# A fused attention and expert kernel: a new written-out order of its work

## The chip, the cores and the metric

The kernel runs on one core of a Trainium2 chip. The core has five engines with a queue each: PE (matrix products, results to PSUM), DVE and ACT (both read PSUM and the on-chip memory), POOL (here: loads and masks) and SP (here: stores). Each takes its instructions in the order of its own list and waits at semaphores for what another engine or a transfer has to finish first. The metric is the device time of the whole program in microseconds: a median of 178.3 over three runs of the kernel before (176.12 to 179.82).

## The reference

Two stages, for a batch of 8 with 576 positions. The first is an attention with 8 heads of 64, whose keys and values are means over groups of 8 positions (576 become 72):

```python
k_p = k.reshape(B, H, Sp, pool, D).mean(axis=3)
v_p = v.reshape(B, H, Sp, pool, D).mean(axis=3)
scores = scale * np.matmul(q, k_p.transpose(0, 1, 3, 2))
...
return np.matmul(attn, v_p)
```

Its output x (8 x 576 x 512) goes through four causal attention experts, of which each position uses the two with the largest gate:

```python
logits = x @ w_gate
topk = np.argpartition(-logits, K, axis=-1)[..., :K]
...
for e in range(E):
    q, k, v = x @ wq[e], x @ wk[e], x @ wv[e]
    scores = np.where(causal, -1e9, scale * (q @ k.transpose(0, 2, 1)))
    ...
    ye = a @ v @ wo[e]
    out += (gate weight of e, or 0) * ye
```

## The kernel before, in words

The batches are worked one after the other, but overlapping: while the experts of one batch run, the first attention of the next two or three is under way. All operations stand as tokens in one string, SEQ, and a loop over it issues them; the order in SEQ is the order in every engine's list, and no scheduler changes it. The semaphores between engines are put in from the data that the operations share. A token is a name, its arguments, the batch behind the colon, a PSUM bank (or a pair) behind the @, and a letter d where DVE is to do what otherwise ACT does. The names, with their lines:

- L_k, L_q, L_v (L118): loads of raw K, V (three each a batch) and q (four), cast to bf16 on the way, issued by POOL. Three raw buffers of each kind go round. In the kernel before the four loads of q of batch 0 are cut in halves, L_q00 to L_q31. W (L131) are the loads of the weights. The loads take eight semaphores in turn, so that each waits for the load eight before it to have landed.
- PK, PV: products on PE that form the means of K and V; kc and vc bring them out of PSUM. KT, kt: K turned on PE, and its copy. u (L251): q turned on DVE, one half of the heads each.
- E0, E1, E2: scores of the first attention (two groups of heads, then the tail of both); e (L277, L270): their exponentials on ACT. D, d, x: sums of the exponentials on PE, then ln and exp(-ln) on ACT (L298, L302). O, o: product with V, and scaling into x transposed on DVE (L321, L314).
- c0 to c4 (L177): weights put into the order that the products read, in the kernel before on ACT.
- P, p: projections to q and k of the experts. V, v: values and gate. g: the gate's small operations on DVE.
- S, s (L437, L431): scores of the experts for pair ep and column group ti (as in S02), and their exponentials on ACT; a (L454, L446): the causal masks on the diagonal blocks, on POOL. B with bz, bg, b: product with V on PE (for a pair and a part of the rows), normalisation and gate on DVE. A product B needs the masks of the diagonal blocks that its rows touch.
- T, t: turning for the last product. Y, y: the last product and its copy to a store buffer, from which SP (at the very end ACT too) stores.
- H (L174): n products of a zero tile of 512 columns, without a use for their result.
- I, J, K, M: constants and padding.

POOL's list thus holds loads and masks in one row: a mask that stands behind a load isn't done before that load is issued. The loop that reads a token ends so:

```python
            elif name == "H":
                warm_up(*a, int(bank))
            ...
            elif name in MATRIX:
                where = tuple(int(x) for x in bank) if name == "E" else int(bank)
                at[b, name, a] = where
                cut[0] = bool(tiled)
                MATRIX[name](b, where, *a)
```

## Time and profile before

| | us |
|---|---|
| median of three runs | 178.3 (176.12 to 179.82) |
| profiled execution | 177.88 |
| its span | 176.2 |
| PE busy in it | 153.7 |
| ACT busy | 140.4 |
| DVE busy | 125.4 |
| POOL busy | 92.8 |

The span runs from the first to the last instruction on the core; the time of an execution is a little longer. Matrix products are pipelined, so a busy PE need not be PE at its peak: the clock that it was granted stands in a row of its own, in tenths of full speed. "Idle before" names who released an engine that waited. A row of a timeline gives start, length, engine, line, operation, output and input, and how many instructions are merged; a row of groups gives busy time and the mean of one instruction in ns. In the list of transfers the last number is the time from issue to landing.

### The profile page before, as it was taken

The numbers are of one execution on the slowest core, as the hardware profiler recorded it, in microseconds if no ns is written. First come the engines' busy times: TensorE is split into PE (matmuls) and PEld (weight loads), VectorE is DVE, ScalarE is ACT, GpSimd is POOL, SyncE is SP. The second block draws the span as 40 slices with busy tenths as digits, with TensorE's granted clock in tenths as the row PEclk, the third lists the DMA queues.
The fourth block names the chain that finished last, engine by engine and source line by source line (L and its number), as shares of the span: only waits on it lengthen the run. The fifth ranks groups of instructions, "written<-read, shape, count | busy, mean of one in ns | idle before, by whom it ended". The sixth has DMA issues, their size and how long they took to land.

```text
span 176.2 us, 5231 instructions
## 1 busy us (share of the span) xinstructions
PE 153.7 (87%) x2028; PEld 83.9 (48%) x2028; DVE 125.4 (71%) x404; ACT 140.4 (80%) x257; POOL 92.8 (53%) x166
## 2 busy tenths in 40 slices
PE   7288798998950899999999999999999999989960
PEld 2023343454520474754455656664457556546630
DVE  1330433594860579898999999999888769999960
ACT  2025989999970388999999999989899999989760
POOL 7889577677597988977468402401303054422000
PEclk9957999999998589999999999999999999999999
DMA  3999999999999998999999921002011020169894
GB/s 31 166 104 155 179 180 180 179 185 181 180 181 180 173 119 85 142 193 211 209 181 209 182 66 61 4 0 65 0 63 60 30 93 6 70 242 347 274 339 168
DMA packets 65577, 24.99 MB, mean 142 GB/s; under 512 B 60688, under 2 KB 60944, under 8 KB 65552
## 3 DMA queue, kind: packets, MB, share of 16 engines
q0 software_dynamic: 60304, 15.21, 88.2%
q1 hardware_dynamic: 5024, 9.05, 14.6%
q10 hardware_dynamic: 224, 0.39, 0.7%
q8 instruction: 16, 0.26, 0.6%
q14 instruction: 9, 0.07, 0.1%
HBM read 30.42 MB, written 9.44 MB: 226 GB/s over the span
## 4 chain that ended last, share of the span: by engine, by line
PE 60%; ACT 12%; DVE 10%; DMA 7%; issue 4%; POOL 2%; ACTq 0%; DVEq 0%; POOLq 0%
PE psum L186 54%; DMA vraw<-in_v_dram 4%; DMA kraw<-in_k_dram 4%; PE psum L195 3%; ACT etb L437 3%; ACT eta L277 3%; PE psum L174 3%; DVE ofin L177 2%; ACT rza L302 2%; ACT rza L298 2%; DVE qk L177 1%; POOL kraw L118 1%; DVE osc L493 1%; DVE gt L488 1%; POOL vraw L118 1%
## 5 line engine op out<-in xcount | busy, mean ns | idle before, releaser
L437 ACT ACTIVATE etb<-psum 128x1024 bf16<-128x1024 f32 x48 | 46.8, 1032 | 1.8 <-PE psum L186 1.4
L454 POOL TENSOR_SCALAR_AFFINE_SELECT etb<-etb 128x256 bf16<-128x256 bf16 x64 | 25.0, 409 | 39.6 <-ACT etb L437 39.0
L277 ACT ACTIVATE eta<-psum 96x1024 bf16<-96x1024 f32 x32 | 31.1, 1022 | 2.5 <-PE psum L186 2.3
L186 PE MATMUL psum<-vaug,etb 128*128 128x65 bf16 x480 | 21.1, 195 | 7.2 <-POOL etb L454 6.6
L118 POOL DMA_DIRECT2D qraw<-in_q_dram x36 | 23.3, 655 | 5.2 <-DMA vraw<-in_v_dram 1.6
L186 PEld LDWEIGHTS <-etb 128*128 128x128 bf16 x480 | 18.7, 99 | 14.1 <-POOL etb L454 7.3
L186 PE MATMUL psum<-wvg,xT 128*128 128x260 bf16 x144 | 22.0, 285 | 0.6 <-ACT wvg L177 0.5
L118 POOL DMA_DIRECT2D kraw<-in_k_dram x24 | 18.6, 781 | 7.2 <-PE psum L186 2.3
L118 POOL DMA_DIRECT2D vraw<-in_v_dram x24 | 18.5, 772 | 6.7 <-PE psum L186 2.1
L177 DVE CAST qk<-psum 128x512 bf16<-128x512 f32 (+1 forms) x26 | 17.0, 653 | 7.0 <-PE psum L186 5.9
L321 DVE TENSOR_TENSOR xT<-psum,rza 128x512 bf16<-128x512 f32 x32 | 20.6, 682 | 1.5 <-ACT rza L302 1.3
L186 PE MATMUL psum<-wop,oT 128*128 128x512 bf16 (+1 forms) x74 | 20.1, 373 | 0.2 <-DVE qk L177 0.2
L186 PE MATMUL psum<-xT,wkp 128*128 128x512 bf16 (+1 forms) x128 | 19.4, 286 | 0.3 <-ACT eta L277 0.3
L186 PE MATMUL psum<-xT,wqp 128*128 128x512 bf16 (+1 forms) x128 | 19.5, 286 | 0.1
L493 DVE TENSOR_TENSOR osc<-psum,gt 128x256 bf16<-128x256 f32 (+2 forms) x40 | 16.9, 424 | 1.4
L186 PEld LDWEIGHTS <-xT 128*128 128x128 bf16 x144 | 13.0, 100 | 8.2 <-issue 4.9
L186 PE MATMUL psum<-qk 64*128 64x64 bf16 (+4 forms) x192 | 16.1, 284 | 0.4 <-DVE kp L177 0.3
L177 ACT COPY ofin<-psum 128x512 f32<-128x512 f32 (+1 forms) x24 | 13.9, 590 | 3.1 <-PE psum L186 2.1
L251 DVE STREAM_TRANSPOSE qT<-qraw 128x576 f32<-128x576 f32 x16 | 12.0, 765 | 5.4 <-DMA qraw<-in_q_dram 5.4
L186 PE MATMUL psum<-qT,kpT 32*96 32x512 bf16 (+1 forms) x256 | 13.7, 312 | 0.6 <-ACT etb L437 0.6
L486 DVE RECIPROCAL rzb<-psum 128x4 f32<-128x4 f32 (+2 forms) x40 | 6.8, 173 | 9.3 <-PE psum L186 8.4
L174 PE MATMUL psum<-warm 128*128 128x512 bf16 x34 | 12.0, 498 | 1.6 <-DVE onesd L147 1.3
(78 smaller groups left out, 240.2 us busy)
## 6 DMA issues: line engine op xcount, KB each, us to landing
out_dram<-ofin SPq DMA_DIRECT2D x31, 256.0 KB, 3.4
kraw<-in_k_dram POOLq DMA_DIRECT2D x24, 192.0 KB, 7.6
vraw<-in_v_dram POOLq DMA_DIRECT2D x24, 192.0 KB, 7.3
qraw<-in_q_dram POOLq DMA_DIRECT2D x28, 144.0 KB, 7.9
out_dram<-ofin SPq DMA_DIRECT2D x7, 128.0 KB, 2.8
qraw<-in_q_dram POOLq DMA_DIRECT2D x8, 72.0 KB, 4.7
wst_q<-in_moe_wq_dram POOLq DMA_DIRECT2D x1, 256.0 KB, 6.6
wst_k<-in_moe_wk_dram POOLq DMA_DIRECT2D x1, 256.0 KB, 7.4
```

Source lines behind the costliest of these rows:

```text
L118: nc.gpsimd.dma_start(out=dst, in_=src)
L174: nc.tensor.matmul(out=psum[:, bank, :], lhsT=warm[:, 0:128], rhs=warm[:], start=True, stop=True)
L177: (nc.vector.tensor_copy if dve else nc.scalar.copy)(out=out, in_=in_)
L186: nc.tensor.matmul(out=out, lhsT=lhsT, rhs=rhs, start=start, stop=stop)
L195: nc.tensor.transpose(out=out[s], in_=in_[:, s], identity=ident[0:n, 0:n])
L251: nc.vector.transpose(out=dst.rearrange("p (a s n) -> p a n s", s=32, n=2), in_=src.rearrange("p (a n d) -> p a n d", n=2, d=32))
L277: nc.scalar.activation(out=eta[:, h : h + 3 : 2, 0:MAIN], in_=psum[0:KR, bank : bank + 2, :], func=EXP, scale=ATT_EXP_SCALE,)
L321: nc.vector.tensor_tensor(out=xT[:, 2 * g + t, mcols(b)], in0=psum[:, bank, :], in1=rz[:, g, 0:MAIN], op=MULT)
L437: nc.scalar.activation(out=et[:, ep, :, eo : eo + n], in_=psum[:, bank : bank + 2, 0:n], func=EXP, scale=MOE_EXP_SCALE,)
L454: nc.gpsimd.affine_select(out=blk, in_=blk, pattern=[[0, 2], [1, 128]], compare_op=ISGE, fill=0.0, base=0, channel_multiplier=-1,)
L486: nc.vector.reciprocal(out=rz, in_=o[:, :, :, HD : HD + 1])
L493: nc.vector.tensor_tensor(out=oscs[ep][:, own, :].rearrange("p c (e d) -> p e c d", e=2), in0=o[:, :, :, 0:HD], in1=gt.to_broadcast([128, ...
```

## The change

SEQ is replaced by another order of nearly the same tokens. What differs in kind:

- q of batch 0 comes in four loads, as for the other batches, not in eight halves.
- The weights' loads W1 to W4 stand elsewhere: W1 behind K of batch 1, W2 to W4 ahead of K of batch 2.
- c0 to c4 carry the d: DVE does them.
- Eighteen H products stand first on PE, then 3 and 10 around the turning of K; 39 in all instead of 34. A new mark c on an H token makes the product small: only the last 32 rows of the bank are written.
- Masks stand singly between loads: from batch 0 on, a row of loads is broken by the masks that are ready there.
- B10 of batch 0 stands ahead of PV of batch 2 and PK of batch 3; before, B00 was the first product B, behind PK of batch 3.
- The rest is placed anew all the way through, with other PSUM banks and other shares of ACT and DVE in the copies. The last tokens, from the last row of blocks on, are nearly the same.

```diff
--- before.py
+++ after.py
@@ -169,9 +169,10 @@
             nc.vector.memset(etbs[1 - h][64 * h : 64 * h + 64, :, :, 1536:1600], 0.0)
 
 
-    def warm_up(n, bank):
+    def warm_up(n, bank, low):
+        rows = slice(KR, 128) if low else slice(0, 128)
         for _ in range(n):
-            nc.tensor.matmul(out=psum[:, bank, :], lhsT=warm[:, 0:128], rhs=warm[:], start=True, stop=True)
+            nc.tensor.matmul(out=psum[rows, bank, :], lhsT=warm[:, rows], rhs=warm[:], start=True, stop=True)
 
     def copy(dve, out, in_):
         (nc.vector.tensor_copy if dve else nc.scalar.copy)(out=out, in_=in_)
@@ -553,73 +554,72 @@
              "d": (dn, "D"), "o": (ov, "O"), "v": (vg, "V"), "p": (p, "P"), "s": (sb, "S"),
              "t": (t, "T"), "y": (y, "Y")}
...
-        I:0 L_k0:0 L_k1:0 L_k2:0 J:0 K:0 M:0 L_q00:0 L_q10:0 H8:0@0 L_q20:0 L_q30:0 L_q01:0 L_q11:0 L_q21:0 PK:0@0
-        L_q31:0 H3:0@1 L_v0:0 kc:0 KT:0@0 L_v1:0 u0:0 H2:0@1 kt:0 L_v2:0 E0:0@02 W0:0 H7:0@4 e01:0 W1:0 u1:0 e00:0
-        L_k0:1 E1:0@24 E2:0@06 L_k1:1 e21:0 e10:0 L_k2:1 e20:0 L_q0:1 D0:0@2 e11:0 PV:0@3 L_q1:1 D2:0@0 d0:0 D1:0@1
-        vc:0d L_q2:1 H1:0@4 x0:0 c0:0 O01:0@3 L_q3:1 d1:0 O00:0@2 O20:0@4 o01:0 O10:0@5 x1:0 O11:0@6 L_v0:1 H8:0@1
-        o00:0 d2:0 x2:0 L_v1:1 o11:0 o10:0 L_v2:1 c1:0 P_q0:0@5 L_k0:2 c2:0 o20:0 c3:0 L_k1:2 P_k0:0@4 p_q0:0 L_k2:2
-        P_t0:0@6 p_k0:0 PK:1@5 L_q0:2 p_t0:0 S00:0@0 L_q1:2 kc:1 S03:0@2 S01:0@6 s03:0 KT:1@5 L_q2:2 s00:0 S02:0@2
-        kt:1d H5:0@4 L_q3:2 s01:0 u0:1 W2:0 s02:0 u1:1 E0:1@04 W3:0 e01:1 E1:1@26 W4:0 e11:1 L_v0:2 P_k1:0@4 L_v1:2
-        e10:1 D1:1@5 p_k1:0d PV:1@6 L_v2:2 d1:1 P_q1:0@7 vc:1d e00:1 L_k0:3 E2:1@24 O10:1@6 p_q1:0d L_k1:3 x1:1 O11:1@0
-        D0:1@1 e21:1 o11:1 L_k2:3 PK:2@7 e20:1 d0:1 D2:1@2 O01:1@3 o10:1 L_q0:3 O00:1@0 d2:1 O20:1@1 x2:1 S12:0@4 kc:2d
-        x0:1 L_q1:3 o20:1 s12:0 S11:0@6 o01:1 L_q2:3 P_t0:1@1 o00:1 s11:0 S10:0@2 L_q3:3 KT:2@4 u0:2 P_k1:1@0 p_t0:1
-        L_v0:3 kt:2 u1:2 s10:0 P_k0:1@1 L_v1:3 c4:0 p_k1:1 L_v2:3 E1:2@46 p_k0:1d V3:0@2 L_k0:4 e11:2 V2:0@0 v3:0d
-        L_k1:4 V2:1@1 e10:2 v2:0d E0:2@26 v2:1d L_k2:4 V1:0@0 e01:2 L_q0:4 V0:0@1 v1:0d P_q0:1@4 e00:2 L_q1:4 v0:0d
-        g1:0 E2:2@06 L_q2:4 g2:0 g0:0 D1:2@5 p_q0:1 g3:0 PV:2@2 g4:0 g5:0 e21:2 L_q3:4 g6:0 D0:2@4 e20:2 g7:0 V0:1@3
-        vc:2d d0:2 L_v0:4 V1:1@0 d1:2 v0:1d V3:1@4 L_v1:4 g8:0 x1:2 g9:0 S03:1@2 v1:1d S02:1@6 O10:2@5 x0:2 a02:0 v3:1d
-        O00:2@0 O01:2@1 s03:1 o10:2 a00:0 PK:3@4 s02:1 a01:0 O11:2@2 o01:2 D2:2@5 a12:0 P_q1:1@3 kc:3 o00:2 L_v2:4 d2:2
-        o11:2 B00:0@1 V4:1@0 p_q1:1 a11:0 bz00:0 S00:1@4 bg00:0 a10:0 b00:0 v4:1 S12:1@2 S10:1@6 u0:3 a03:0 s00:1
-        V3:2@1 L_k0:5 g1:1 B01:0@0 g2:1 v3:2 L_k1:5 KT:3@4 g3:1 s10:1 V0:2@5 g4:1 bz01:0 bg01:0 P_q0:2@1 b01:0 a02:1
-        v0:2d s12:1 kt:3d a10:1 B12:0@0 p_q0:2d L_k2:5 V1:2@4 g0:1 x2:2 S11:1@2 bz12:0 g5:1 v1:2 a12:1 S01:1@6 g6:1
-        g7:1 T01:0@1 s11:1 g8:1 B10:0@5 g9:1 P_k1:2@4 a00:1 bg12:0 t01:0d b12:0 a03:1 bz10:0 s01:1 bg10:0 a11:1 b10:0
-        E0:3@02 L_q0:5 p_k1:2d B02:0@5 e01:3 u1:3 T12:0@6 a01:1 P_k0:2@7 L_q1:5 bz02:0 e00:3 bg02:0 B11:0@4 b02:0
...
-        Y3:7@7 ya4:7 yb4:7d Y2:7@6 y3:7 y2:7dp z2:7
+        I:0 H18:0@0 L_k0:0 L_k1:0 L_k2:0 J:0 K:0 M:0 L_q0:0 L_q1:0 L_q2:0 L_q3:0 L_v0:0 L_v1:0 L_v2:0 PK:0@0 W0:0
+        H3:0@1 kc:0 L_k0:1 KT:0@0 H10:0@1 L_k1:1 kt:0 L_k2:1 u0:0 W1:0 u1:0 E0:0@02 L_q0:1 E1:0@46 e00:0 H3:0@0c L_q1:1
+        e11:0 PV:0@0 L_q2:1 e10:0 H2:0@0c vc:0d e01:0 D0:0@1 c0:0d O01:0@0 L_q3:1 O00:0@4 c1:0d d0:0 D1:0@5 E2:0@26
+        x0:0 L_v0:1 O11:0@1 d1:0 o01:0 e21:0 L_v1:1 O10:0@5 x1:0 o00:0 e20:0 o10:0 O20:0@4 L_v2:1 D2:0@0 PK:1@2 o11:0
+        d2:0 kc:1 P_q0:0@5 x2:0 c2:0d W2:0 o20:0 P_k0:0@2 c3:0d p_q0:0 W3:0 P_t0:0@4 p_k0:0 W4:0 KT:1@5 p_t0:0 kt:1d
+        S00:0@0 L_k0:2 S02:0@2 P_k1:0@5 s00:0 u1:1 L_k1:2 s02:0 u0:1 a00:0 E1:1@06 L_k2:2 p_k1:0d H2:0@4 e10:1 a02:0
+        E0:1@24 e11:1 L_q0:2 H1:0@2c PV:1@0 L_q1:2 e00:1 P_q1:0@1 vc:1d e01:1 E2:1@26 L_q2:2 c4:0d D0:1@0 e20:1 O01:1@4
+        L_q3:2 p_q1:0d d0:1 D1:1@5 V2:0@2 e21:1 L_v0:2 d1:1 V1:0@3 v2:0d x0:1 V0:0@6 L_v1:2 v1:0d x1:1 S10:0@0 o01:1
+        D2:1@2 O11:1@3 v0:0 O00:1@5 d2:1 L_v2:2 V3:0@7 o11:1 x2:1 s10:0 O20:1@2 o00:1 O10:1@6 PK:2@3 L_k0:3 o20:1 v3:0
+        S03:0@4 S11:0@0 kc:2d P_t0:1@2 s03:0 L_k1:3 s11:0 o10:1 V4:1@7 L_k2:3 KT:2@3 p_t0:1d S01:0@4 v4:1 kt:2d S12:0@0
+        g1:0 L_q0:3 P_k1:1@2 s01:0 g2:0 u0:2 L_q1:3 s12:0 P_k0:1@3 u1:2 a10:0 E0:2@46 p_k1:1 L_q2:3 p_k0:1d g0:0 V1:1@0
+        a11:0 e00:2 g3:0 P_q0:1@1 g4:0 L_q3:3 v1:1d e01:2 g5:0 a12:0 E1:2@24 g6:0 g7:0 g8:0 L_v0:3 B10:0@0 g9:0 p_q0:1d
+        e10:2 V3:1@6 bz10:0 PV:2@7 L_v1:3 bg10:0 b10:0 e11:2 D0:2@1 vc:2d a03:0 V2:1@2 L_v2:3 d0:2 v3:1d T10:0@0 V0:1@3
+        v2:1d a01:0 x0:2 E2:2@46 t10:0d O10:2@1 L_k0:4 v0:1d e21:2 D1:2@0 O01:2@2 e20:2 g1:1 O11:2@3 d1:2 L_k1:4
+        O00:2@6 o01:2 D2:2@7 PK:3@4 x1:2 o00:2 L_k2:4 P_q1:1@0 d2:2 kc:3 o10:2 L_q0:4 x2:2 B01:0@2 o11:2 p_q1:1 S00:1@4
+        L_q1:4 g0:1 S02:1@6 u0:3 S11:1@0 s00:1 P_q0:2@3 u1:3 L_q2:4 s02:1 V0:2@4 bz01:0 bg01:0 a00:1 P_k1:2@5 b01:0
+        s11:1 L_q3:4 v0:2d p_q0:2d T01:0@2 a02:1 KT:3@4 p_k1:2 S03:1@6 S12:1@0 kt:3d B12:0@3 s03:1 L_v0:4 t01:0d g2:1
+        s12:1 S10:1@4 bz12:0 S01:1@6 g3:1 L_v1:4 PV:3@2 g4:1 g5:1 s10:1 g6:1 O20:2@0 P_k0:2@1 a03:1 vc:3d L_v2:4 s01:1
+        o20:2 B11:0@2 g7:1 a12:1 g8:1 B02:0@0 p_k0:2 g9:1 bz11:0 E0:3@46 bg11:0 L_k0:5 b11:0 B00:0@1 bg12:0 bz02:0
+        e00:3 P_q1:2@2 b12:0 L_k1:5 bz00:0 bg02:0 bg00:0 b02:0 b00:0 PK:4@3 e01:3 L_k2:5 p_q1:2d E1:3@04 L_q0:5 kc:4d
+        V2:2@2 e10:3 L_q1:5 u0:4 P_t0:2@3 a11:1 T00:0@6 v2:2d B01:1@7 p_t0:2 L_q2:5 t00:0d e11:3 T12:0@0 T11:0@1
+        T02:0@2 D0:3@3 t12:0d t11:0d a10:1 Y1:0@6 t02:0d bz01:1 d0:3 L_q3:5 bg01:1 KT:4@2 b01:1 V3:2@4 y1:0 kt:4d a01:1
...
+        T11:7@7 t12:6d t01:7d y0:7 Y4:7@0 t11:7d Y3:7@3 ya4:7 yb4:7d Y2:7@2 y3:7 y2:7dp z2:7
...
@@ -639,7 +639,7 @@
             elif name == "z":
                 z(b, *a, nc.scalar)
             elif name == "H":
-                warm_up(*a, int(bank))
+                warm_up(*a, int(bank), bool(tiled))
             elif name in "IJK":
                 setup_consts("IJK".index(name))
             elif name == "M":
```

## The prediction

> **What bounds the kernel now.** First the page: its shares, then its forty slices of 4.4 us.

> ```profile
> span 176.2 us, 5231 instructions
> ...
> PE 153.7 (87%) x2028; PEld 83.9 (48%) x2028; DVE 125.4 (71%) x404; ACT 140.4 (80%) x257; POOL 92.8 (53%) x166
> ...
> PE   7288798998950899999999999999999999989960
> ...
> PEclk9957999999998589999999999999999999999999
> DMA  3999999999999998999999921002011020169894
> ```

> The shares name PE, but the slices tell more: from the fifteenth slice on PE is full, and what is lost is lost ahead of it (slices 1 to 4, a zero in slice 13) and in the last two. The granted clock is low in slices 3 and 4 and again in 13 and 14, each time after PE stood still. The DMA engines are full up to slice 22. So I cut the span into stages at events of the trace: K of batch 0 landed (9.33), the first projection (23.66), the pooling of K of batch 3 (49.23), the end of the hole (57.66), the last matmul (170.42). The columns are length, busy time of PE, of PE's weight loads, DVE, ACT and POOL, then clock, DMA share and GB/s.

> ```profile
> 0.00:9.33 9.33, 4.35 (x11) 1.32 (x12) 2.45 (x17) 1.28 (x1) 7.08 (x15) 0.95 1.05 102
> 9.33:23.66 14.33, 12.39 (x116) 4.67 (x115) 4.88 (x8) 9.56 (x17) 11.77 (x16) 0.79 1.54 149
> 23.66:49.23 25.57, 23.76 (x293) 11.94 (x295) 15.41 (x45) 24.46 (x44) 17.57 (x25) 1.00 1.80 181
> 49.23:57.66 8.43, 1.85 (x27) 0.80 (x20) 2.35 (x4) 2.51 (x6) 7.04 (x13) 0.91 1.82 180
> 57.66:63.00 5.34, 5.27 (x43) 3.22 (x44) 3.06 (x13) 2.77 (x7) 5.12 (x11) 0.50 1.54 150
> 63.00:70.00 7.00, 6.80 (x84) 3.81 (x82) 6.42 (x24) 5.58 (x11) 6.11 (x12) 1.00 1.07 104
> 70.00:110.00 40.00, 39.98 (x624) 22.69 (x623) 37.52 (x115) 38.62 (x72) 23.32 (x41) 1.00 1.31 162
> 110.00:153.00 43.00, 42.73 (x638) 25.42 (x637) 37.26 (x118) 40.31 (x73) 11.58 (x29) 1.00 0.11 35
> 153.00:170.42 17.42, 16.54 (x209) 9.98 (x207) 15.38 (x66) 14.72 (x32) 3.18 (x8) 1.00 0.84 296
> 170.42:176.20 5.78, 0.00 (x1) 0.00 (x0) 0.69 (x1) 0.58 (x1) 0.00 (x0) 0.95 0.57 194
> ```

> Each stage has its own limit. Up to 23.66 a chain over all engines begins with the first loads. From 23.66 to 49.23 it is ACT (24.46 of 25.57 busy) with the DMA queue close behind at a steady 181 GB/s. Then comes a hole: 8.43 us in which PE works 1.85, so 6.58 idle. After it PE runs 5.34 us at half its clock, and from 63 on PE is the limit, idle only 0.20 + 0.02 + 0.27 + 0.88 = 1.4 us until the last matmul. The timelines of PE and POOL, one row of ACT's and one piece of the chain of waits say what the hole is.

> ```profile
> 50.04 1.04 PE L186 MATMUL psum<-xT,wqp 128*128 128x512 bf16 x4
> 57.66 0.76 PE L186 MATMUL psum<-vaug,etb 128*128 128x65 bf16 x6 [6.58 <-POOL etb L454]
> ...
> 39.31 1.06 ACT L437 ACTIVATE etb<-psum 128x1024 bf16<-128x1024 f32 x1
> ...
> 47.27 6.77 DMA vraw<-in_v_dram
> ...
> 54.61 0.77 POOL L118 DMA_DIRECT2D vraw<-in_v_dram  x1 [0.70 <-DMA vraw<-in_v_dram]
> 55.68 0.77 POOL L118 DMA_DIRECT2D vraw<-in_v_dram  x1 [0.30 <-issue]
> 56.45 2.22 POOL L454 TENSOR_SCALAR_AFFINE_SELECT etb<-etb 128x256 bf16<-128x256 bf16 x6
> ```

> PE stands before B00:0, the first product of the second attention, which needs the causal masks of batch 0. ACT had the last exponentials of that batch ready at 40.4. The masks are POOL's, and POOL works in order: ahead of them stood loads, each waiting until the load eight before it has landed. At 54.61 it still waits for a V load; only at 56.45 come six masks in 2.22 us. So the masks came some 16 us after their data.

> **The change part by part.** My sum goes along the stages, against the profiled execution's 177.88 us (span 176.2 and 1.68 around it); the median of the runs shown, 178.3, is 0.4 us above it.

> *The start.* These rows, of PE, DVE and ACT, carry it.

> ```profile
> 1.26 3.60 PE L174 MATMUL psum<-warm 128*128 128x512 bf16 x8 [1.26 <-DVE onesd L147]
> 9.33 1.01 PE L186 MATMUL psum<-kraw,poolk 96*32 96x512 bf16 x4 [2.41 <-DMA kraw<-in_k_dram]
> 21.67 1.89 PE L174 MATMUL psum<-warm 128*128 128x512 bf16 x8 [0.34 <-ACT rza L298]
> ...
> 12.52 0.78 DVE L251 STREAM_TRANSPOSE qT<-qraw 128x576 f32<-128x576 f32 x1 [0.87 <-DMA qraw<-in_q_dram]
> ...
> 13.98 1.93 ACT L277 ACTIVATE eta<-psum 96x1024 bf16<-96x1024 f32 x2 [1.41 <-PE psum L186]
> 19.34 0.61 ACT L298 ACTIVATE rza<-psum 128x512 f32<-128x512 f32 x1
> ```

> Eighteen warm-ups stand first in place of eight. Eight took 3.60 us cold and eight 1.89 us at full clock; some eight at 0.45 and ten at 0.24 end near 7.3, before K has landed at 9.33, so they block nothing. They take away the long idle time after which slices 3 and 4 ran slow. With K at 9.33 the four left pooling matmuls (0.5 at full clock instead of 1.01), kc and the flips end near 10.8; then ten warm-ups by 0.24 hold PE until 13.2. The q loads are four instead of eight: the same bytes and half the issues, but the first turn now waits for both halves. At 9.33 us 0.95 MB had moved (102 GB/s); K and q of a batch are 1.18 MB, so at 149 to 181 GB/s they are through near 10.8, landed near 12, and two turns by 0.78 end at 13.5. So E0 starts at 12.8 to 13.2, is over near 13.9, and the exponentials begin where they do now (13.98): nothing gained, and 1 us lost if q lands a microsecond later.

> Behind that the order changes. Now six exponentials stand ahead of d0 at 19.34, with waits for cold PE work between them; in the new order four stand there, by 0.95 some 3.9 us: d0 at 18.0, 1.3 us earlier. The weight casts c0 to c4 leave ACT for DVE:

> ```profile
> L177 ACT COPY wqp<-wst_q 128x512 bf16<-128x512 bf16 x2 | 1.2, 602 | 0.0
> L177 ACT COPY wkp<-wst_k 128x512 bf16<-128x512 bf16 x2 | 1.1, 613 | 0.0
> L177 ACT COPY wvg<-wst_v 128x1024 bf16<-128x1024 bf16 x1 | 1.1, 1074 | 0.0
> L177 ACT COPY wvg<-wst_g 128x16 bf16<-128x16 bf16 x1 | 0.2, 243 | 0.0
> ```

> One of them, 0.6, stands between x0 and d1 in the chain. P_q0:0 thus starts some 2.0 us earlier, at 21.7; ends 0 (q late) and 3. DVE has room for the casts: 4.88 us busy in 14.33 and 15.41 in 25.57. DVE's price for them isn't in the trace; between nothing and ACT's it changes nothing under that cover.

> *From the first projection to the pooling of K of batch 3.* ACT is the limit, and it loses c2, c3 and the two casts of c4 here: 1.2 + 1.1 + 0.2 = 2.5 us. The rest of its list is much the same: two evictions of q or k, a kc and a kt go, three V evictions come. The queue allows that gain and no more:

> ```profile
> kraw<-in_k_dram POOLq DMA_DIRECT2D x24, 192.0 KB, 7.6
> vraw<-in_v_dram POOLq DMA_DIRECT2D x24, 192.0 KB, 7.3
> qraw<-in_q_dram POOLq DMA_DIRECT2D x28, 144.0 KB, 7.9
> wst_q<-in_moe_wq_dram POOLq DMA_DIRECT2D x1, 256.0 KB, 6.6
> ```

> A batch is 3 x 192 + 4 x 144 + 3 x 192 = 1728 KB, the weights 1028; up to K of batch 3 that is 3 x 1728 + 1028 + 576 = 6788 KB or 6.95 MB. From 0.95 MB at 9.33, at 181 GB/s, it is there at 42.5; if the dip to 149 GB/s before 23.66 recurs, 2.5 us later. ACT would come there at 49.23 - 2.0 - 2.5 = 44.7, between the two. I take -2.5; ends 0 and -3.5.

> *The hole.* Between the loads the list of POOL now has masks. B10:0 comes first, ahead of V of batch 2, and needs the masks a10 and a11 of batch 0; these stand behind two loads of q of batch 3 and a third, which wait for the last of q and the first of v of batch 2. Bytes to there: 2 x 1728 + 1152 + 192 + 1028 = 5828 KB, 5.97 MB: 9.33 + 5.02 / 0.181 = 37.1, or 39.6 with the dip, and about 1 us for issue and mask. PE gets there with 5.6 us of ACT's work still to do before K of batch 3, at 39 to 40. The wait is thus between 0 and 2 us, not 6.58. B00:0 comes only some 13 us later. No load behind them waits longer on that account: a mask is 2.22 / 6 = 0.37 us and the queue has eight loads in it. I take the 6.58 off, and the slow clock with it: 5.27 us at 0.50 hold 2.6 us of work. Together -9.2; ends 0, where the same hole is somewhere else, and -9.2.

> [...]

> *What is late next.* From K of batch 3 to the last matmul PE works 1.85 + 5.27 + 6.80 + 39.98 + 42.73 + 16.54 = 113.2 us, 110.6 at full clock; the tokens behind that point are nearly the same ones (31 projections in both, 49 score groups for 47, 27 V for 28, 39 products B for 40). That it could be fed with 1.4 us of idle time was helped by the hole, in which loads ran on. Without it ACT has about 105 us to do in those 112, DVE little less, and three engines so close will wait for one another. I add 2 us; ends 0 and 7. The loads don't limit it: 1.77 MB a batch take 9.8 us, PE needs some 17. SP's stores are the same forty, behind the same evictions, and the last 5.78 us, stores included, are the same tokens.

> Sum: 177.9 - 2.0 - 2.5 - 9.2 + 2.0 = **166.2**. From the other side: 44.7 + 110.6 + 1.4 + 2.0 + 5.8 + 1.7 = 166.2.

> **The rivals.**

> *Half the gain.* The loads set the pace up to batch 3 and PE waits for them and for the masks behind them: the queue dips as it does now (149 GB/s), K of batch 3 is there at 45 to 47, B10:0 waits 2 us, and the later masks, again placed between waiting loads (batch 1's behind q and v of batch 4), cost 2 to 3 more. For it: POOL is still in order and every load still waits for one. Against: the bytes are as early as PE. 166.2 + 5 = 171.

> *No change.* The hole only moves: PE is as late at its next bound, ACT and the loads. 178. Against it: 6.58 us in which ACT was idle too (2.51 busy of 8.43), and loads twice as fast as PE.

> *Slower.* One mechanism: the masks of B10:0. Now PE first needs a mask at 51.1 (50.04 + 1.04), in the new order at 39 to 40. If the loads ahead of the masks land x us late, PE stands there for x and the slow clock (2.6) is back; and the queue being late by as much, it comes again at the masks of batch 1, likewise between loads: 166.2 + 2 (x + 2.6). It decides from x = 5 (181.4, 2% above); at the 6.58 of now it gives 184.6. Nothing in the rows shows such a delay at a steady 181 GB/s.

> *The change doesn't do what it says*: the lists of instructions show the masks between the loads, so that falls under the second.

> **How the numbers follow.** 0.62 for the forecast (162 to 169), 0.23 for half the gain (169 to 174), 0.08 for no change, 0.07 for slower. The predicted time is 166; from 161.5 to 174 are the first two, with 0.16 left out and a little below. The low end is all ends at their best: 177.9 - 3 - 3.5 - 9.2 = 162.2. Two per cent, about what a measurement of this kernel can tell from no change, is 3.6 us: faster 0.86, same 0.07, slower 0.07.

> **What would show it.** PE without an idle time over 3 us between 13 and 150 us, the granted clock at 1.00 from 6 us on; P_q0:0 near 21.7, K of batch 3 pooled near 44.7, B10:0 near 40 with under 2 us of wait for POOL; last matmul near 158. I am wrong if a wait of PE for masks or K/V loads over 3 us stands between 25 and 60, if ACT waits long for PE before 45, or if PE is idle by more than 6 us in all behind 45.

## The result and the profile after

The kernel after takes 163.32 us (median of four runs, 163.03 to 163.7) against 177.75 for the kernel before beside it (176.12 to 179.82): a ratio of 0.922, with a 95% interval of 0.914 to 0.929. That is 13.9 us less by the ratio, where 12 had been forecast. The profiled execution took 163.38 us. Here and below, ratios leave out a run over 1.5% longer than the quickest of its kernel, while medians and ranges keep it.

The page of the kernel after: span, shares, and the forty slices, now 4.04 us each.

```profile
span 161.7 us, 5222 instructions
...
PE 150.5 (93%) x2033; PEld 83.1 (51%) x2033; DVE 124.1 (77%) x411; ACT 136.3 (84%) x250; POOL 90.4 (56%) x162
...
PE   6896699899999999999999999999999999999950
...
PEclk9999858999999999999999999999999999999996
DMA  2999999999999999999999920101141122357894
```

The zero of slice 13 is gone, and PE is full from the ninth slice on. Two things differ from what was expected: PE is not quite full before that, and the clock is low again, in slices 5 to 7. I cut the span at the same events as before, this time K of batch 0 at 8.32, the first projection at 20.95, the pooling of K of batch 3 at 46.78 and the last matmul at 155.75. The columns are length, busy PE, weight loads, DVE, ACT, POOL, then clock, DMA share and GB/s.

```profile
0.00:8.32 8.32, 6.30 (x21) 2.27 (x21) 2.45 (x17) 1.28 (x1) 7.09 (x15) 1.00 0.99 95
8.32:20.95 12.63, 9.97 (x118) 3.86 (x118) 5.18 (x10) 7.75 (x13) 9.73 (x13) 0.92 1.81 179
20.95:46.78 25.83, 25.37 (x305) 12.30 (x305) 17.64 (x54) 22.69 (x42) 21.48 (x34) 0.91 1.80 181
46.78:155.75 108.97, 108.90 (x1606) 64.68 (x1598) 98.18 (x331) 104.01 (x194) 52.07 (x102) 1.00 0.92 146
155.75:161.70 5.95, 0.01 (x1) 0.00 (x0) 0.69 (x1) 0.59 (x1) 0.00 (x0) 0.75 0.66 224
```

The same cut of the kernel before, in one row for the fourth stage:

```profile
49.23:170.42 121.19, 113.17 (x1614) 65.92 (x1607) 101.98 (x335) 104.51 (x196) 56.35 (x112) 0.97 0.85 133
```

So the fourth stage gave 12.2 us of the 14.5 by which the span is shorter; the first two together 2.7, the third nothing (25.83 for 25.57), the tail lost 0.2. In the fourth, PE is idle for 0.07 us in 109. The timelines of POOL and PE around the place of the old hole:

```profile
38.98 0.42 POOL L455 TENSOR_SCALAR_AFFINE_SELECT etb<-etb 128x256 bf16<-128x256 bf16 x1
39.34 0.66 POOL L118 DMA_DIRECT2D qraw<-in_q_dram  x1
40.00 0.42 POOL L455 TENSOR_SCALAR_AFFINE_SELECT etb<-etb 128x256 bf16<-128x256 bf16 x1
...
42.61 0.36 PE L187 MATMUL psum<-vaug,etb 128*128 128x65 bf16 x6
...
46.78 0.62 PE L187 MATMUL psum<-kraw,poolk 96*32 96x512 bf16 x6
```

The two masks that B10:0 needs come singly between loads of q and are done at 40.4; PE reaches B10:0 at 42.61 and has no wait in its row. Before, six masks stood behind a V load until 56.45.

### The profile page after: what moved, and what is told of

It is laid out like the page before. It is cut to its first block, busy times and chain, and to the rows that moved or that the text cites. A ratio compares the mean times of both kernels' runs of the same rounds, so it can differ in the third digit from the quotient of the medians.

```text
span 161.7 us, 5222 instructions
## 1 busy us (share of the span) xinstructions
PE 150.5 (93%) x2033; PEld 83.1 (51%) x2033; DVE 124.1 (77%) x411; ACT 136.3 (84%) x250; POOL 90.4 (56%) x162
## 4 chain that ended last, share of the span: by engine, by line
PE 80%; ACT 8%; DMA 3%; POOL 3%; issue 1%; DVE 1%; ACTq 0%; POOLq 0%; DVEq 0%
PE psum L187 76%; ACT eta L278 5%; PE psum L196 4%; DMA qraw<-in_q_dram 3%; ACT etb L438 2%; POOL kraw L118 2%; POOL qraw L118 1%; ACT rza L299 1%; DVE qT L252 0%; ACT rza L303 0%; ACT eta L271 0%; ACT ofin L178 0%; ACTq L545 0%; DVE ofin L178 0%; ACT etb L432 0%
## 5 line engine op out<-in xcount | busy, mean ns | idle before, releaser
L455 POOL TENSOR_SCALAR_AFFINE_SELECT etb<-etb 128x256 bf16<-128x256 bf16 x64 | 25.5, 411 | 46.0 <-ACT etb L438 45.2
L118 POOL DMA_DIRECT2D qraw<-in_q_dram x32 | 21.3, 669 | 2.5 <-DMA wst_q<-in_moe_wq_dram 0.8
L187 PE MATMUL psum<-wvg,xT 128*128 128x260 bf16 x144 | 20.9, 275 | 0.0
L187 PE MATMUL psum<-xT,wqp 128*128 128x512 bf16 (+1 forms) x128 | 20.8, 297 | 0.0
L187 PE MATMUL psum<-xT,wkp 128*128 128x512 bf16 (+1 forms) x128 | 20.6, 297 | 0.0
L187 PE MATMUL psum<-vaug,etb 128*128 128x65 bf16 x480 | 20.5, 193 | 0.0
L118 POOL DMA_DIRECT2D kraw<-in_k_dram x24 | 18.6, 780 | 2.5 <-PE psum L187 1.2
L118 POOL DMA_DIRECT2D vraw<-in_v_dram x24 | 18.5, 773 | 2.1 <-DMA kraw<-in_k_dram 1.4
L178 ACT COPY ofin<-psum 128x512 f32<-128x512 f32 (+1 forms) x26 | 14.8, 585 | 1.8 <-PE psum L187 1.2
L178 DVE CAST qk<-psum 128x512 bf16<-128x512 f32 (+1 forms) x23 | 14.8, 649 | 1.3 <-PE psum L187 1.1
L252 DVE STREAM_TRANSPOSE qT<-qraw 128x576 f32<-128x576 f32 x16 | 11.7, 757 | 5.3 <-DMA qraw<-in_q_dram 5.3
L187 PE MATMUL psum<-eta,vp 96*32 96x512 bf16 (+1 forms) x256 | 13.3, 292 | 1.5 <-ACT eta L271 0.6
L187 PE MATMUL psum<-qT,kpT 32*96 32x512 bf16 (+1 forms) x256 | 13.5, 305 | 0.6 <-DVE qT L252 0.4
L187 PEld LDWEIGHTS <-wqp 128*128 128x128 bf16 x128 | 8.6, 101 | 8.7 <-issue 4.0
## 6 DMA issues: line engine op xcount, KB each, us to landing
out_dram<-ofin SPq DMA_DIRECT2D x31, 256.0 KB, 3.0
kraw<-in_k_dram POOLq DMA_DIRECT2D x24, 192.0 KB, 7.4
qraw<-in_q_dram POOLq DMA_DIRECT2D x32, 144.0 KB, 7.4
vraw<-in_v_dram POOLq DMA_DIRECT2D x24, 192.0 KB, 7.3
wst_q<-in_moe_wq_dram POOLq DMA_DIRECT2D x1, 256.0 KB, 7.2
wst_k<-in_moe_wk_dram POOLq DMA_DIRECT2D x1, 256.0 KB, 8.6
wst_v<-in_moe_wv_dram POOLq DMA_DIRECT2D x1, 256.0 KB, 7.5
```

What stands on the lines that cost most here:

```text
L118: nc.gpsimd.dma_start(out=dst, in_=src)
L178: (nc.vector.tensor_copy if dve else nc.scalar.copy)(out=out, in_=in_)
L187: nc.tensor.matmul(out=out, lhsT=lhsT, rhs=rhs, start=start, stop=stop)
L252: nc.vector.transpose(out=dst.rearrange("p (a s n) -> p a n s", s=32, n=2), in_=src.rearrange("p (a n d) -> p a n d", n=2, d=32))
L455: nc.gpsimd.affine_select(out=blk, in_=blk, pattern=[[0, 2], [1, 128]], compare_op=ISGE, fill=0.0, base=0, channel_multiplier=-1,)
```

## The experiments

Ratios are to the kernel before, run on the same chip beside each kernel. In the diffs the tokens of SEQ stand without their line breaks, with "..." for what is between.

**The place of the masks alone (e2, e1).** In e2, the kernel before, with the seven masks of batch 0 together at the first place at which all their data exists.

```diff
-... KT:2@4 ... u1:2 s10:0 P_k0:1@1 L_v1:3 ... x0:2 a02:0 v3:1d ... a00:0 PK:3@4 ... a01:0 ... a12:0 ... a11:0 ... a10:0 ... a03:0
+... KT:2@4 ... u1:2 s10:0 a02:0 a00:0 a01:0 a12:0 a11:0 a10:0 a03:0 P_k0:1@1 L_v1:3 ... x0:2 v3:1d ... PK:3@4 ...
```

> The kernel before, with the seven masks of batch 0 moved up in the order to just behind the last exponential of that batch (token s10:0); nothing else. Theory: POOL does them near 45.5 to 48.5, ahead of B00:0 at 51.1, so the 6.58 us of PE's idle time and the 2.6 us of slow clock go and at most 2 us of new waits come: 177.8 - 9.2 + 1.5 = 170 (168 to 172), with the clock at 1.00 from 50 to 70. Rival (the hole only moves to the next wait, at the masks of batch 1 or the loads behind): 175 to 178, with a new wait of PE over 4 us before 75.

It took 170.55 us (170.12 to 172.16), ratio 0.960 (0.954 to 0.967). Timelines of POOL and PE:

```profile
44.40 2.94 POOL L454 TENSOR_SCALAR_AFFINE_SELECT etb<-etb 128x256 bf16<-128x256 bf16 x8
...
49.90 0.40 PE L186 MATMUL psum<-kraw,poolk 96*32 96x512 bf16 x3
```

The masks are through at 47.3, the hole is gone, the clock stays at 1.00 there, and 7.1 us of the 13.9 (both by the ratios) come with seven tokens that moved. The other 6.8 are the question of all that follows.

The opposite, e1, was tried in the kernel after: fourteen loads, of q and V of batch 3 and of K, q and V of batch 4, ahead of mask a10 of batch 0 instead of among the masks.

```diff
-... u1:2 a10:0 ... L_q2:3 ... L_q3:3 ... L_v0:3 B10:0@0 ... L_v1:3 ... L_v2:3 ... L_k0:4 ... L_v1:4 ...
+... u1:2 L_q2:3 L_q3:3 L_v0:3 L_v1:3 L_v2:3 L_k0:4 L_k1:4 L_k2:4 L_q0:4 L_q1:4 L_q2:4 L_q3:4 L_v0:4 L_v1:4 a10:0 ... B10:0@0 ...
```

> The changed kernel, with the fourteen loads from q of batch 3 to v of batch 4 moved ahead of mask a10 of batch 0; nothing else moves. Theory (the gain of the hole comes from masks that don't stand behind waiting loads): the masks a10 and a11 come only when the loads ahead of them are issued, near 50 us, so B10:0 waits for POOL from 42.6 to about 51, PE restarts at half its clock for some 5 us, and the time is 163.3 + 8.5 + 2.6 = 174 (170 to 177). Rival (the new order as a whole, with its other work ahead and casts on DVE, makes the gain; the place of the masks matters little): PE waits under 3 us there and the time is 164 to 167.

It took 177.64 us (176.84 to 178.54), ratio 1.002 (0.998 to 1.005): with all else new in place, the whole gain is gone. Timelines of POOL and PE:

```profile
51.96 0.77 POOL L118 DMA_DIRECT2D vraw<-in_v_dram  x1 [0.68 <-DMA vraw<-in_v_dram]
53.04 0.77 POOL L118 DMA_DIRECT2D vraw<-in_v_dram  x1 [0.31 <-issue]
53.81 1.50 POOL L455 TENSOR_SCALAR_AFFINE_SELECT etb<-etb 128x256 bf16<-128x256 bf16 x4
...
54.29 0.76 PE L187 MATMUL psum<-vaug,etb 128*128 128x65 bf16 x6 [12.39 <-POOL etb L455]
```

PE stands 12.39 us at B10:0, and then has a mean clock of 0.53 over 3.71 us (54.29 to 58.00), by which 1.74 us of it are lost. The two make 14.1 us, and the kernel is 14.3 slower by the medians, so nearly all of the price is accounted for. The theory had said 170 to 177; the price is a little above its upper end. The place of the masks in POOL's list is thus worth between 7 us and all of it, depending on what stands ahead of them.

**The casts (e3, e8, e11).** In e3, the kernel after with c0 to c4 back on ACT.

```diff
-... c0:0d ... c1:0d ... c2:0d ... c3:0d ... c4:0d ...
+... c0:0 ... c1:0 ... c2:0 ... c3:0 ... c4:0 ...
```

> The changed kernel with the weight casts c0 to c4 on ACT again. By the prediction's steps they cost ACT 1.2 us in the start and 2.5 us up to the pooling of K of batch 3: 163.3 + 0.6 + 2.5 = 166.4 (165 to 167.5). Rival (ACT isn't the limit of that stage in the changed kernel: it idles 3.1 us there, waiting for projections at half clock): 163.3 to 164.5.

166.32 us (165.11 to 167.12), ratio 0.934 (0.928 to 0.939): 3.0 us more by the medians, 2.1 by the ratios. ACT's timeline, then one row of it in the kernel after, and for DVE's price the groups of the kernel after:

```profile
17.52 1.14 ACT L178 COPY wqp<-wst_q 128x512 bf16<-128x512 bf16 x2
18.54 0.61 ACT L299 ACTIVATE rza<-psum 128x512 f32<-128x512 f32 x1
...
23.06 1.12 ACT L178 COPY wkp<-wst_k 128x512 bf16<-128x512 bf16 x2
```

```profile
16.79 0.61 ACT L299 ACTIVATE rza<-psum 128x512 f32<-128x512 f32 x1
```

```profile
L178 DVE COPY wkp<-wst_k 128x512 bf16<-128x512 bf16 x2 | 0.6, 309 | 0.2 <-DMA wst_k<-in_moe_wk_dram 0.2
L178 DVE COPY wqp<-wst_q 128x512 bf16<-128x512 bf16 x2 | 0.5, 292 | 0.0
```

The casts stand ahead of d0 (L299), whose start slips from 16.79 to 18.54. Of these 1.75 us, 0.66 are there already when K of batch 0 lands (8.98 for 8.32), so 1.1 are the casts. From the first projection to K of batch 3 this execution took 26.24 us, 0.4 more than the kernel after, although ACT had its casts of the stage again (c2 and c3 from 23.06, 1.12 us); its mean granted clock, though, was 0.985, in the kernel after 0.970. DVE does one cast in 0.29 to 0.31 us, where ACT took 0.60. So within the new order the casts are worth 2 to 3 us by the times, of which the trace, from the quickest of the four executions, shows about 1.1 ahead of d0; where the rest comes in the others was not seen.

Then, in e8, the same move in the old order, with the masks already in place:

```diff
 the diff of the masks alone, and
-... c0:0 ... c1:0 ... c2:0 ... c3:0 ... c4:0 ...
+... c0:0d ... c1:0d ... c2:0d ... c3:0d ... c4:0d ...
```

> The kernel before with the seven masks of batch 0 moved ahead of its waiting loads (as in e2_masks_early) and c0 to c4 given to DVE. Theory: the place of the masks (7.2 us by e2) and the casts (3.0 by e3) are separate costs at separate places, so they add up: 177.7 - 7.2 - 3.0 = 167.5 (166.8 to 168.5). Rival: the casts are worth 3 us only in the new order, where ACT's list ahead of d0 is shorter; in the old order six exponentials still stand ahead of d0 and the loads catch up, so that 169.5 to 170.5 is left.

172.43 us (170.23 to 173.4), ratio 0.970 (0.962 to 0.977), no faster than without the casts (0.954 to 0.967): the sum of the two did not come. The profiled execution took 173.4 us, the longest of the four, so its lines are read for the place of a wait and not for its size. Its timelines of PE and POOL:

```profile
46.83 0.40 PE L186 MATMUL psum<-kraw,poolk 96*32 96x512 bf16 x3
62.54 0.79 PE L186 MATMUL psum<-vaug,etb 128*128 128x65 bf16 x12 [3.04 <-POOL etb L454]
...
61.29 0.77 POOL L118 DMA_DIRECT2D kraw<-in_k_dram  x1
62.06 1.13 POOL L454 TENSOR_SCALAR_AFFINE_SELECT etb<-etb 128x256 bf16<-128x256 bf16 x3
```

PE came to batch 3 some 3 us earlier than in e2 (46.83 for 49.90) and then stood at the masks of batch 1, which wait behind loads of K as those of batch 0 had behind loads of V. The time gained was returned at that stop. Not all of it came from the casts: 1.9 us of it were there at the first projection (21.15 for 23.06), ahead of which only c0 and c1 differ, but PE ran slowly for longer at the start of e2: eight first scores and the seven warm-ups behind them took 1.09 and 2.45 us there, in e8 0.76 and 1.69. In e11 below, where they took 1.09 and 2.19, batch 3 comes 1.8 us earlier than in e2. To see whether that stop alone was to blame, in e11 the masks of batch 1 of that kernel were also moved to their exponentials, and five loads that had stood around them behind the last mask:

```diff
-... s03:1 ... s02:1 ... L_v2:4 ... s00:1 ... L_k0:5 ... L_k1:5 ... s10:1 ... a02:1 ... s12:1 ... a10:1 ... L_k2:5 ... a12:1 ... s11:1 ... a00:1 ... a03:1 s01:1 ... a11:1 ... a01:1
+... s03:1 a03:1 ... s02:1 a02:1 ... s00:1 a00:1 ... s10:1 a10:1 ... s12:1 a12:1 ... s11:1 a11:1 ... s01:1 a01:1 L_v1:4 L_v2:4 L_k0:5 L_k1:5 L_k2:5 ...
```

> e8_masks_casts with the masks of batch 1 placed early too: each directly behind its exponentials, and the two V and three K loads that stood around them (L_v1:4 to L_k2:5) behind the last one. Theory: with the casts on DVE the old order came to batch 3 some 3 us earlier (K pooled at 46.83 instead of 49.90 in e2) and gave it back at the masks of batch 1, where PE stood 3.04 us and lost its full clock; without that stop the casts are worth their 3 us here too: 167.5 (166.5 to 168.5). Rival: behind the masks stands another bound of the old order (the loads, or ACT), so that 169.5 to 172.5 stays.

171.28 us (170.41 to 172.73), ratio 0.971 (0.961 to 0.980). The theory fell. No mask holds PE at 62 any more; PE's timeline shows the next one:

```profile
48.14 0.40 PE L186 MATMUL psum<-kraw,poolk 96*32 96x512 bf16 x3
...
76.40 0.38 PE L186 MATMUL psum<-vraw,poolv 96*32 96x512 bf16 x1 [0.42 <-DMA vraw<-in_v_dram]
77.49 0.59 PE L186 MATMUL psum<-vraw,poolv 96*32 96x512 bf16 x4 [0.72 <-DMA vraw<-in_v_dram]
```

and between 70 and 110 us PE is idle for 2.8 us, in the kernel before for 0.02:

```profile
70.00:110.00 40.00, 37.17 (x542) 21.03 (x545) 36.32 (x106) 35.72 (x63) 22.72 (x42) 1.00 1.22 150
```

These are waits for V of batch 5, whose loads the edit did not move: PE comes to it at 75.6, 2.3 us earlier than in e2 (77.9), but its last two loads are issued at 67.1 and 68.3, hardly earlier than in e2 (67.8 and 68.6). The two waits are 1.1 of the 2.8 us; another 0.97, at 96.4, is one for DVE that e2 has too (0.90). In these traces of the old order a stop taken out is followed by another a little further on.

**The first q in four loads, and the warm-ups (e7, e9, e12, e4).** In e7, the kernel after with q of batch 0 in halves again:

```diff
-... M:0 L_q0:0 L_q1:0 L_q2:0 L_q3:0 L_v0:0 ...
+... M:0 L_q00:0 L_q10:0 L_q20:0 L_q30:0 L_q01:0 L_q11:0 L_q21:0 L_q31:0 L_v0:0 ...
```

> The changed kernel with q of batch 0 in eight half loads again. By the prediction's step q was the last thing ahead of E0 (turned at 11.64 to 13.08). With halves the first turn can go when the first four have landed, near 10.6, but the second comes later, since POOL issues twice as often (eight by 0.6 instead of four by 0.67, 2.2 us more) and the loads of v and the weights stand behind. The ten warm-ups hold PE until 12.1, so E0 begins at 12.1 instead of 12.48, and E1 waits for the second turn: 163.0 to 164.0, no difference that counts. Rival (four loads instead of eight carry a good part of the 2.7 us gained in the start): 164.5 to 165.5.

165.42 us (163.59 to 166.95), ratio 0.930 (0.925 to 0.935): 2.1 us more by the medians (1.8 without the 166.95), 1.5 by the ratios, so the rival's time was right. The profiled execution took only 163.84 and shows only where it can come from. POOL's timeline, of this kernel and then of the kernel after:

```profile
4.08 4.24 POOL L118 DMA_DIRECT2D qraw<-in_q_dram  x7
...
9.14 2.31 POOL L118 DMA_DIRECT2D vraw<-in_v_dram  x3
```

```profile
4.07 2.66 POOL L118 DMA_DIRECT2D qraw<-in_q_dram  x4
6.72 2.31 POOL L118 DMA_DIRECT2D vraw<-in_v_dram  x3
```

A half costs POOL 0.61 us to issue, nearly as much as a whole load (0.66); V of batch 0 and all that follows is issued 2.4 us later. In that execution PE waited 1.03 us for V and 0.59 for K of batch 1, and came to K of batch 3 0.44 us later (47.22). How much of the difference in the median lies there was not seen. In these six it went with the clock: the two executions with a mean granted clock of 0.985 took 163.59 and 163.84, hardly more than the kernel after, and the four with 0.957 to 0.966 took 165.08 to 166.95. Why the halves should lead to more time at half clock is not shown.

The same in the old order: e9 is e8 with this step and eighteen warm-ups, e12 is e11 with it and eight:

```diff
-... M:0 L_q00:0 L_q10:0 H8:0@0 L_q20:0 L_q30:0 L_q01:0 L_q11:0 L_q21:0 PK:0@0 L_q31:0 ...
+... M:0 L_q0:0 L_q1:0 L_q2:0 L_q3:0 H18:0@0 PK:0@0 ...
```

> The same, with the first q in four loads and eighteen warm-ups at the outset in place of eight. Theory: q in four loads is worth the 2.1 us by which the halves slowed the new order (e7), so 165 to 166.3, and what is left to the 163.3 of the kernel after is its replanned order behind the first projections. Rival: in the old order the halves cost nothing, since the six exponentials ahead of d0 set the pace: as e8 within 0.5 us.

> The same with the first q in four loads (eight warm-ups as in the kernel before). Theory: half the issues ahead of the first exponentials, as in e7, where undoing it cost 2.1 us: 165 to 166.5. Rival: in the old order nothing waits for them: within 0.7 of e11.

170.44 us (168.92 to 171.12), ratio 0.963 (0.959 to 0.968), and 172.41 (171.68 to 173.8), ratio 0.977 (0.969 to 0.985). Against the kernels without this step (0.970 and 0.971) the intervals overlap, and the two go opposite ways: 1.1 us less by the ratios (2.0 by the medians) in e9, 1.0 more in e12. So no gain is shown in the old order, but one of 1 to 2 us with eighteen warm-ups is not excluded. A reason may be that its first scores are laid out to begin on the first half of q; that was not tested. Against the masks alone (0.960) the masks, casts, four loads and eighteen warm-ups of e9 together (0.963) bring nothing more. PE's first projections come at 24.48 and 23.72, later than in e11 (22.60), which has q in halves.

In e4, the kernel after, the warm-ups were cut from 18 and 10 to 8 and 2:

```diff
-I:0 H18:0@0 L_k0:0 ... KT:0@0 H10:0@1 L_k1:1 ...
+I:0 H8:0@0 L_k0:0 ... KT:0@0 H2:0@1 L_k1:1 ...
```

> The changed kernel with 8 warm-ups at the outset instead of 18, and 2 instead of 10 behind the turning of K. Theory: PE stands still from 4.9 to 8.3 but for the first poolings, the clock falls to half near 8.5 as in the kernel before, and the poolings, flips and first scores run slow: the exponentials begin 0.5 to 1 us later than 13.16 and the time is 163.8 to 164.5. Rival (the clock's early state doesn't matter, since q is late anyway): 163.0 to 163.6.

163.74 us (162.81 to 165.17), ratio 0.921 (0.915 to 0.926): no difference that can be told. PE's timeline:

```profile
13.19 1.95 PE L187 MATMUL psum<-qT,kpT 32*96 32x512 bf16 x16 [1.03 <-DVE qT L252]
...
21.62 1.04 PE L187 MATMUL psum<-xT,wqp 128*128 128x512 bf16 x3
```

The first scores run slowly (1.95 for 16, in the kernel after 1.31), but the projections run fast (1.04), where in the kernel after four took 1.89. In this execution the slow stretch lasted from the start to about 17 us (one product took 0.63 at 16.22, three took 0.47 at 17.21), instead of the start to 5.2 and then 18.8 to 25.6: it changes its place.

**What sets the stage from 21 to 47 us (e5, e6, e10).** In the kernel after the clock is at half for 6.8 us, from 18.8 to 25.6 (windows of the kernel after):

```profile
16.00:18.00 2.00, 1.91 (x35) 0.78 (x35) 0.69 (x3) 1.97 (x5) 1.07 (x2) 1.00 1.82 180
18.00:19.40 1.40, 0.45 (x4) 0.10 (x3) 1.30 (x3) 1.40 (x5) 1.08 (x2) 0.79 1.82 181
19.40:20.95 1.55, 1.29 (x30) 0.55 (x31) 1.33 (x3) 0.48 (x2) 0.82 (x2) 0.50 1.82 180
20.95:22.60 1.65, 1.65 (x7) 0.58 (x5) 0.89 (x3) 0.79 (x2) 1.00 (x2) 0.50 1.80 182
22.60:24.30 1.70, 1.70 (x5) 0.60 (x4) 0.00 (x0) 0.59 (x1) 1.52 (x3) 0.50 1.82 179
24.30:25.40 1.10, 1.10 (x20) 1.06 (x19) 0.00 (x0) 0.59 (x1) 1.10 (x2) 0.50 1.82 180
25.40:26.20 0.80, 0.80 (x11) 0.34 (x9) 0.37 (x2) 0.49 (x2) 0.23 (x1) 0.85 1.82 181
```

In e5 six warm-ups in the sparse stretch ahead of it were to keep the clock:

```diff
-... L_v0:1 O11:0@1 ... o10:0 O20:0@4 ...
+... L_v0:1 H3:0@3 O11:0@1 ... o10:0 H3:0@3 O20:0@4 ...
```

> The changed kernel with three full warm-up products put ahead of O11:0 and three ahead of O20:0, where PE stands still between 17.9 and 19.7, so that the clock should not fall to half at 19.4. Theory (the half clock from 19.4 to 25.4 took back the 2.5 us that the casts gave ACT): the clock row shows 1.00 from 6 us on, K of batch 3 is pooled near 44.5 and the time is 163.3 - 2.4 = 161 (160.5 to 161.5). Rival (the loads or ACT set that stage anyway, the slow clock lies beside them): 162.5 to 163.8, with new waits of ACT or PE for loads before 47.

163.5 us (162.47 to 165.5), ratio 0.920 (0.916 to 0.924). The clock stood at 1.00 in every window from 8.32 to 155.75, and the time is that of the kernel after; the 2.4 us expected did not come. Timelines of DVE, PE and ACT:

```profile
26.18 1.44 DVE L252 STREAM_TRANSPOSE qT<-qraw 128x576 f32<-128x576 f32 x2 [1.41 <-DMA qraw<-in_q_dram]
...
27.02 0.66 PE L187 MATMUL psum<-qT,kpT 32*96 32x512 bf16 x8 [1.03 <-DVE qT L252]
...
27.71 3.76 ACT L278 ACTIVATE eta<-psum 96x1024 bf16<-96x1024 f32 x4 [0.99 <-PE psum L187]
```

PE, now faster, waits for q of batch 1; the scores of batch 1 begin at 27.02, in the kernel after at 27.19. K of batch 0 had landed 0.59 us later here (8.91); counted from there, the full clock brings these scores 0.76 us nearer and K of batch 3 0.43, and that is all. With fourteen warm-ups instead of six, e6, it was the same:

```diff
-... L_v0:1 O11:0@1 ... L_v1:1 O10:0@5 ... o10:0 O20:0@4 ... D2:0@0 PK:1@2 ...
+... L_v0:1 H4:0@3 O11:0@1 ... L_v1:1 H4:0@3 O10:0@5 ... o10:0 H4:0@3 O20:0@4 ... D2:0@0 H2:0@3 PK:1@2 ...
```

> The same with four warm-up products ahead of O11:0, O10:0 and O20:0 each and two ahead of the pooling of K of batch 1: 14 in all. If six were too few to hold the clock, these do it and give the 161 expected of the six; if the clock was held by six already, these add up to 1 us of PE work in the chain: 161.5 to 162.5. Rival as for the six: 163 to 164.5.

163.9 us (163.1 to 166.05), ratio 0.924 (0.921 to 0.928).

That made the loads look like the limit, so in e10 one load of 256 KB was put ahead of q of batch 1:

```diff
-... u1:0 E0:0@02 L_q0:1 ... x2:0 c2:0d W2:0 o20:0 ...
+... u1:0 E0:0@02 W2:0 L_q0:1 ... x2:0 c2:0d o20:0 ...
```

> The kernel after with one load of the weights, W2 (256 KB), moved ahead of q of batch 1. Theory: the loads set the pace from 20 to 47 us (scores of batch 1 begin near 27 whatever PE's clock is), so 0.26 MB at 180 GB/s, 1.45 us, put ahead of that q delay those scores to 28.5 and K of batch 3 behind them, 164.3 to 164.8. Rival: ACT's list sets the pace there and the loads have slack: 163.0 to 163.7.

164.02 us (163.75 to 164.21), ratio 0.926 (0.922 to 0.930), 0.7 us more by the medians and 0.8 by the ratios, between the two expectations and with overlapping intervals. PE's timeline:

```profile
8.80 0.59 PE L187 MATMUL psum<-kraw,poolk 96*32 96x512 bf16 x4 [0.93 <-DMA kraw<-in_k_dram]
...
27.80 0.66 PE L187 MATMUL psum<-qT,kpT 32*96 32x512 bf16 x8
...
47.35 0.61 PE L187 MATMUL psum<-kraw,poolk 96*32 96x512 bf16 x6
```

The scores of batch 1 are 0.61 us late, and 0.48 of it is there already when K of batch 0 lands (8.80 for 8.32), ahead of the edit. So the loads alone don't set the stage either: at half clock PE is as late as the loads are, within a microsecond, and each of the two hides what is done to the other. A kernel with the full clock and an earlier q at once was not run.

## Why the prediction was right, and where it wasn't

The total lay inside the forecast: 163.3 where 166 was said. That it came within 3 us is in part luck: two of the five terms were far off, one by 2.8 us too hopeful and one by 5.0 too cautious. The steps, against the two profiled executions (176.2 and 161.7 us of span):

| step | forecast | profile |
|---|---|---|
| start, to the first projection | -2.0 | -2.7 |
| first projection to K of batch 3 | -2.5 | +0.3 |
| the hole and the slow clock behind it | -9.2 | -9.2 |
| "what is late next" | +2.0 | -3.0 |
| tail | 0 | +0.2 |
| sum | -11.7 | -14.5 |

The two -9.2 are the same figure: it is what the kernel before lost at the hole (6.58 idle and 2.6 at half clock), all of which is gone, and the -3.0 is the rest of the 12.2 of the fourth stage.

*The start* was right in its mechanism and 0.7 us too small. K of batch 0 landed at 8.32 for 9.33, which is more than that difference and varies between executions (8.3 to 9.0 in the variants of the kernel after). Measured from there, the stage is 12.63 us for 14.33, 1.7 shorter, where the shorter list ahead of d0 and a cast were worked out to 1.9. The four loads of q were booked at nothing gained; e7 puts 1.5 us or more of the whole time on them, and the forecast had not looked at V, which is issued earlier behind them. q landed at 11.64 and the exponentials began at 13.16, 0.8 before the forecast. The sign "the granted clock at 1.00 from 6 us on" did not hold: the clock fell at about 18.8.

*To K of batch 3* the term of -2.5 was wrong. ACT did lose its casts (22.69 busy for 24.46), but the step took ACT as the limit of the whole stage. In its first 5 us ACT now waits for PE at half clock (2.34 busy of 5.05, which was one of the forecast's own signs of being wrong), and behind the half clock stands q of batch 1; e5 and e10 show that the two end within a microsecond of each other. In e3 the casts put back on ACT made this stage only 0.4 us longer, not 2.5. From 26 us on ACT is full (20.35 of 20.78 us). PK:3 was forecast at 44.7 and came at 46.78. I had bounded the loads only by K of batch 3, at the end of the stage (42.5 to 45), not by q of batch 1, near its beginning.

*The hole* went as forecast, and e1, which brings it back, bears out the mechanism. B10:0 came at 42.61, later than the 39 to 40 said, since the stage ahead was longer, and waited 0 us (0 to 2 said). e2 shows that this step needs none of the rest, e1 that all the rest is worth nothing without it. The forecast took the slow clock from one row, 5.34 us at 0.50, which is the part of the stretch in which PE worked. In the kernel before the clock was at half from 56.16 to 62.99, that is from 1.50 us before PE's work began, and in the kernel after from 18.82 to 25.65, each time 6.83 us; PE was busy for 1.85 and 2.81 us of the first half of the stretch and for all of the second.

*"What is late next"* had the wrong sign. It expected 2 us of new waits where the hole had helped the feeding of PE; there are none (108.90 busy of 108.97, where before 1.4 were idle), and the work behind the mark is 1.7 us less (108.9 for 110.6), as some products of both attentions and of V had moved ahead of it. These two make the -3.0. That such a rest was a real danger, the old order shows: with the masks early it needs 113.1 us for the same stage (windows of e2):

```profile
49.90:163.01 113.11, 109.41 (x1594) 64.80 (x1609) 101.67 (x335) 104.06 (x194) 52.86 (x103) 1.00 0.89 142
```

*The rivals.* "Half the gain" and "no change" did not come. The mechanism of "slower", masks behind late loads, did not act here, but e1 shows it is real, at 14.2 us by the ratios for fourteen loads; the wait alone was 12.39. A small slip of reading: the DMA shares before are full up to slice 23, not 22; nothing rests on it.

What stays open: which of the many moves in the new order gives the 6.8 us beyond the masks. Where it lies can be read: between the spans of e2 and of the kernel after (168.8 and 161.7), 3.1 us are there at K of batch 3 (49.90 and 46.78) and 4.1 come behind it, 3.6 of them idle time of PE. It is not the casts, the four loads or the warm-ups by themselves as far as can be told, since in the old order none of them showed a gain clear of the scatter. e11 changed the loads together with the masks, so it cannot say that the old order could not be mended otherwise.

## What to carry to other kernels

In a queue that works in order, look first at what cheap work stands behind waiting loads: seven masks of 0.37 us moved in a list were worth half of this gain, and a wrong place for them all of it. Gains need not add up: the casts were worth 2 to 3 us in the new order, where PE ran without a stop to the end, and showed nothing in the old one, where it met another stop. A repaired clock showed nothing with a second limit within a microsecond of it, so the neighbour's time is to be read before a term is booked.

## What the runs showed of the hardware

For the fall these traces show no such order. In the kernel after the clock fell to half at 18.82 us although no single idle time of PE between 14.3 and 19.7 was over 0.61 us; in the step ahead of it PE was busy for 2.19 of 3.42 us. The four wide products of the first projection to k, at 22 to 25 us, take 1.03 us in the two kernels that have more products in that stretch (e5, e6), and 1.28 to 1.91 in the five of the new order without them and with all warm-ups (the kernel after 1.91, e1 1.56, e3 1.74, e7 1.28, e10 1.91). So in the kernel after it wasn't a long gap alone that cost the clock; but in the kernel before a step with only 1.74 of 3.41 us busy (from 49.34) passed without a fall.

And the row of granted clock does not show the slow start of these executions. In the kernel after the page prints 9 in its first slices, ahead of 5.17 us as behind it; but the warm-up products start 0.43 us apart until then and 0.22 behind it (ten busy for 3.91 us from 1.26 on, ten for 2.03 from 5.17 on). In the kernel with few warm-ups (e4, mean granted clock 0.998) the first scores take 1.95 us instead of 1.31, under a row of nothing but nines:

```profile
PEclk9999999999999999999999999999999999999999
```
